# Sliding-window attention and SwiGLU on one core: an earlier first weight load, a rearranged start, and regrouped projection phases

## The chip, the cores and the metric

The kernel runs on one core of a Trainium2 chip. The metric is the device time of one launch in microseconds (us); smaller is better. "Before" is the kernel as it stood, "after" is the kernel with the change.

## The reference

The first half is causal attention with a window of 64 keys, for 8 batches, 8 heads, 576 tokens and a head size of 64. The second half is a SwiGLU block on the 4608 x 512 matrix of attention outputs, with a hidden size of 1536. All inputs and the output are float32.

```python
scores = q @ k.T / sqrt(64)                 # per batch and head
mask = (0 <= i - j) & (i - j < 64)
attn = softmax(where(mask, scores, -1e9))
x = (attn @ v) reshaped to (4608, 512)
g, val = x @ w_gate, x @ w_val              # 512 x 1536 each
out = (g * sigmoid(g) * val) @ w_out        # 1536 x 512
```

## The kernel before

The 4608 tokens are cut into nine tiles of 512, `t` = 0 to 8. Eight of them are the first 512 tokens of a batch. The ninth, `t` = `LAST` = 7, collects the last 64 tokens of all eight batches. Matmuls take bf16 operands and accumulate in float32 in PSUM.

Every tile passes through three steps.

*Attention.* Heads are taken in four pairs, `u` = 0 to 3. `scores(t, u)` makes the scores of a pair with small 64x64 matmuls (line 227), exponentiates them on ScalarE into `E` (line 233), and for `t` > 0 multiplies by a 0/1 mask on VectorE (line 235). `sums(t, u)` adds up the exponentials with two matmuls against a tile of ones (`totals`, line 245), and inverts the sum on ScalarE as exp(-ln(sum)) (lines 253 and 256). `values(t, u)` multiplies by the values with sixteen small matmuls (line 271) and scales the result by the inverse sum on VectorE into `xT` (line 277). `products` is `sums` and then `values`.

*Gate.* `gate_value(t, m)`, for `m` = 0 to 11, does four matmuls of 512 columns with `wg` into `g_ps` and four with `wv` into `v_ps` (line 306). `gate_end` applies SiLU on ScalarE (line 299) and multiplies on VectorE into `hT` (line 300). For `t` = 0 the first two `m` are done in parts by `gate_part` (line 286), one input chunk `c` at a time.

*Projection.* `project(t, s)`, for `s` = 0 to 3, does twelve matmuls of 512 columns with `wo` (line 315). `project_end` copies the result out of PSUM on VectorE (line 322), and SyncE stores it with four DMAs (line 334). For the last tile every other store is issued by ScalarE.

The order is written out by hand (`manual_schedule`): each engine executes its instructions in the order in which the program lists them. In the loop over `t`, the projection of tile `t` - 1 is woven into the attention of tile `t`: two `scores`, a `project`, two `scores`, a `project`, two `products`, a `project`, two `products`, a `project`. Then come the twelve `gate_value` of tile `t`. The text calls the woven part a projection phase.

ScalarE has two tables of functions to switch between: `set_exp` ahead of the scores, `set_silu` ahead of the gate.

The start has an order of its own (lines 351 to 538). Queries and keys of `t` = 0 come in float32 (`raw`), are cast to bf16 by `cast_first` (the table `casts` says which engine takes which; line 408), are turned by TensorE (`turn_pe`), and go through `scores(0, u)`. `keep_warm` puts dummy matmuls into TensorE's gaps. GpSimd casts, and it also issues most DMAs, all into one queue, in this order: two of the values of `t` = 0, the weights `wg` and `wv` in five steps each (`weights_gv`, line 160; with the casts of two value blocks, `cast_v`, after the first `wg`), four DMAs `q_s` with the queries of `t` = 1 (`load_qk(1)`, line 87), `wo` in three steps (`weights_o`, line 166), then values and more queries and keys. ScalarE issues four DMAs `k_f` with the keys of `t` = 1 during the gate of `t` = 0, casts them (`keys`, line 408), and TensorE turns them. The queries of `t` = 1 are turned on VectorE by `turn_q` (line 186), which needs all four `q_s`.

PSUM has four tags with two buffers each way: `a` (two buffers of two banks, for scores, some sums, values and turned keys), and `g` and `v` (two buffers of one bank each, for the gate, the sums of `t` > 0 in `v`, and projections in `g`).

Of the kernel before, what the change touches and what calls it, by code (L numbers as in the profile page):

```python
# [8 lines left out]
P = 128  # L9
FP32 = mybir.dt.float32  # L10
BF16 = mybir.dt.bfloat16
# [6 lines left out]
def kernel(  # L18
# [107 lines left out]
    def load_v(eng, dst, t, which=range(4)):  # L126
        for i in which:
            eng.dma_start(  # L128
                dst[:, i], v[batch(t), :, P * i:P * i + P].rearrange("h r d -> r h d")
            )  # L130
# [27 lines left out]
    def weights_gv(f0, f1, *which):  # L158
        for i in which or range(2):
            nc.gpsimd.dma_start(  # L160
                (wg, wv)[i][:, :, f0:f1],
                (moe_w_gate, moe_w_val)[i][:, f0:f1].rearrange("(c r) f -> r c f", r=P),
            )
# [79 lines left out]
    def totals(t, u, d_ps):  # L243
        for h in range(2):
            nc.tensor.matmul(  # L245
                d_ps[64 * h:64 * h + 64], ones[:, 0:D], weights[t, u][:, h, :]
            )

    def room(n):
        return fsb.tile([P, 2, 512], FP32, name="r", tag="r", bufs=4)[:, 0:n]  # L250

    def log(r, d_ps):
        nc.scalar.activation(r, d_ps, AF.Ln)  # L253

    def invert(r):
        nc.scalar.activation(r, r, AF.Exp, scale=-1.0)  # L256

    def sums(t, u, d_ps):
        totals(t, u, d_ps)
        r = room(1)[:, 0]  # L260
        log(r, d_ps)
        invert(r)
        inverse[t, u] = r

    def values(t, u, o_ps):
        E = weights.pop((t, u))
        if u == 0:
            xT[t] = att.tile([P, 4, 512], BF16, name="xT", tag="xT")
        for m in range(8):
            for h in range(2):  # L270
                nc.tensor.matmul(  # L271
                    blocks(o_ps[64 * h:64 * h + 64], t, m, m + 1),
                    (v1, v2)[m // 4][t % 2][:, m % 4, 2 * u + h, :] if t == LAST
                    else (v2, v1)[m % 2][t % 2][:, m // 2, 2 * u + h, :],
                    blocks(E[:, h, :], t, m, m + 1),
                )
        nc.vector.tensor_mul(xT[t][:, u, :], o_ps[:], inverse.pop((t, u)))  # L277

    def products(t, u):
        sums(t, u, ps_f.tile([P, 512], FP32, name="d_ps", tag="v")[:])  # L280
        values(t, u, ps_a.tile([P, 2, 512], FP32, name="ao_ps", tag="a")[:, 0])

    def gate_part(t, ms, tiles, c):
        for m, pair in zip(ms, tiles):
# [6 lines left out]
    def gate_tiles():  # L291
        return [ps_f.tile([P, 512], FP32, name=x + "_ps", tag=x) for x in "gv"]
# [43 lines left out]
    def out_tile():  # L336
        return ps_f.tile([P, 512], FP32, name="o_ps", tag="g")

    def project(t, s):
        o_ps = out_tile()  # L340
        project_part(t, (s,), (o_ps,), range(12))
        project_end(t, s, o_ps)

    def set_exp():
        nc.scalar.preload_act_table_set("natural_log_exp_and_others")

# [9 lines left out]
        load_runs(nc.scalar if u < 2 else nc.sync, raw[1][:, hs], k, 0, hs)  # L356
    load_v(nc.sync, staged[0, "v"], 0, (0, 1))
    set_exp()
    nc.vector.memset(ones[:], 1.0)
    make_identity(nc, identb[:])  # L360
    nc.vector.memset(zero[:], 0.0)
    for i in range(2):
# [3 lines left out]
    def keep_warm(n):  # L366
        for _ in range(n):
            nc.tensor.matmul(warm[0:D], ones[:, 0:D], ones[:])

    keep_warm(7)  # L370
    nc.gpsimd.memset(tri[:], 1.0)
    for a in range(2):
        half = tri[64 * a:64 * a + 64]
# [27 lines left out]
    def shift_dma(dst, src):  # L401
        nc.sync.dma_start(dst, src)

    def wide(name):
        return ps_a.tile([P, 2, 512], FP32, name=name, tag="a")

    def join(copy, dst, src):
        copy(dst.rearrange("r e (h d) -> r h e d", h=2), src)  # L408

    def one(name):  # L410
        return ps_a.tile([P, 2, 512], FP32, name=name, tag="a")[:, 0]

    casts = ((on_a, on_v), (on_p, on_v), (on_v, on_p), (on_p, on_p))

    def cast_first(u, i):
        join(casts[u][i], first[:, i, u], raw[i][:, 2 * u:2 * u + 2])

    def turn_pe(u):
        tps = [ps_f.tile([P, 512], BF16, name="tp", tag=x) for x in "gv"]
        for i in range(2):  # L420
            transposes(tps[i], first[:, i, u])
        (on_v if u else on_a)(queries[0][:, u, :], tps[0][:])
        split_k(kT[0][:, u, :], tps[1][:])
# [6 lines left out]
    load_v(nc.gpsimd, v1[0], 0, (2, 3))  # L430
    keep_warm(1)
    scores(0, 0)
    cast_first(2, 0)
    turn_pe(1)
    keep_warm(2)
    scores(0, 1)
    cast_first(2, 1)
    turn_pe(2)
    keep_warm(1)
    cast_first(3, 0)  # L440
    cast_first(3, 1)
    scores(0, 2)
    turn_pe(3)
    weights_gv(0, 256, 0)
    cast_v(0, (0, 1))
    weights_gv(0, 256, 1)
    weights_gv(256, 512)
    weights_gv(512, 768)
    weights_gv(768, 1280)
# [3 lines left out]
    weights_o(4, 8)  # L453
    weights_o(8, 12)
    load_v(nc.gpsimd, v1[1], 1)
    d_ps, r = wide("d_ps"), room(2)
    for u in range(2):
        totals(0, u, d_ps[:, u])
        inverse[0, u] = r[:, u]
    log(r, d_ps[:])  # L460
    scores(0, 3)
    invert(r)
    shift_v(0, on_v, 0, 2)
    shift_v(0, on_v, 2, 4)
    keep_warm(3)
    for u in (2, 3):
        d_ps = ps_f.tile([P, 512], FP32, name="d_ps", tag="gv"[u % 2])
        totals(0, u, d_ps[:])
        inverse[0, u] = room(1)[:, 0]
        log(inverse[0, u], d_ps[:])  # L470
    for u in (2, 3):
        invert(inverse[0, u])
    values(0, 0, one("ao_ps"))
    values(0, 1, one("ao_ps"))
    keep_warm(3)
    pairs = [gate_tiles() for _ in range(2)]
    values(0, 2, one("ao_ps"))
    gate_part(0, (0, 1), pairs, 0)
    values(0, 3, one("ao_ps"))
    for c in range(1, 4):  # L480
        gate_part(0, (0, 1), pairs, c)
    set_silu()
    raw_k = stage.tile([P, H, 4, D], FP32, name="k_f", tag="k")
    for m in range(12):
        if m < 2:
            gate_end(0, m, pairs[m])
        else:
            gate_value(0, m)
        if m == 2:
            for i in range(4):  # L490
                nc.vector.tensor_copy(
                    mask[:, 0, :, i], tri[:].rearrange("r c (x e) -> r e c x", e=16)
                )
            nc.vector.memset(mask[64:128, 0, :, 0, 0, :], 0.0)
            nc.vector.tensor_copy(mask[:, 1], mask[:, 0])
        if 3 <= m < 7:
            hs = slice(2 * m - 6, 2 * m - 4)
            load_runs(nc.scalar, raw_k[:, hs], k, 1, hs)
        if 7 <= m < 11:
            u = m - 7  # L500
            join(on_a, keys[:, u], raw_k[:, 2 * u:2 * u + 2])
        if m >= 8:
            u = m - 8
            tp = ps_a.tile([P, 512], BF16, name="tp", tag="a")
            transposes(tp, keys[:, u])
            split_k(kT[1][:, u, :], tp[:])
        if m >= 10:
            turn_q(1, m - 10)
    turn_q(1, 2)
    turn_q(1, 3)  # L510

    set_exp()
# [9 lines left out]
    for i in range(4):  # L522
        shift_v(1, on_v, i, i + 1)

    def d_tile():
        return ps_f.tile([P, 512], FP32, name="d_ps", tag="v")[:]

    for u in range(2):
        sums(1, u, d_tile())
    project(0, 2)  # L530
    o_ps = out_tile()
    for u in range(4):
        if u < 2:
            sums(1, u + 2, d_tile())
        values(1, u, one("ao_ps"))
        if u:
            project_part(0, (3,), (o_ps,), range(4 * u - 4, 4 * u))
    project_end(0, 3, o_ps)

    for t in range(1, NT):  # L540
        if t > 1:
            set_exp()
            for u in range(8):
                if u < 4:
                    scores(t, u)
                else:
                    products(t, u - 4)
                if u % 2:
                    project(t - 1, u // 2)
        set_silu()  # L550
        if t + 1 == LAST:
            load_last_v()
        elif t + 1 < NT:
            if t > 1:
                cast_v(t + 1)
            shift_v(t + 1, shift_dma)
        if t + 2 < NT:
            load_qk(t + 2)
            if t + 2 != LAST:
                stage_v(t + 2)  # L560
        if t == 2:
            k_l = load_k(
                cast.tile([P, 4, 4, 4 * D], BF16, name="k_l", tag="c0"),
                [(b, S - P) for b in range(4, 8)],
            )
            for b in range(8):
                nc.gpsimd.tensor_copy(
                    maskl[:, 0, :, b], tri[:, 1].rearrange("r (x e) -> r e x", e=16)
                )
            nc.gpsimd.tensor_copy(maskl[:, 1], maskl[:, 0])  # L570
        turns = (4, 6, 8, 10) if t == 1 else (1, 4, 7, 10)
        for m in range(12):
            gate_value(t, m)
            if m in turns and t + 1 < NT:
                turn(t + 1, turns.index(m))
            if m == 8 and 3 <= t < 7:
                turn_k(kT[2], k_l, t - 3)
    for s in range(4):
        project(NT - 1, s)

# [1 line left out]
_INS = ['q', 'k', 'v', 'moe_w_gate', 'moe_w_val', 'moe_w_out']  # L582
# [26 lines left out]
```

## Time and profile before

| | us |
|---|---|
| median of 7 runs | 338.07 (337.81 to 339.51) |
| the profiled execution's own time | 339.1 |
| its span in the profile | 337.3 |
| TensorE busy | 324.0 (96% of the span) |
| VectorE busy | 215.4 (64%) |
| ScalarE busy | 167.4 (50%) |
| GpSimd busy | 138.7 (41%) |
| mean granted TensorE clock | 0.994 of full speed |

The busy shares are averages over the span. The chain of waits, the idle time ahead of each instruction and the order of instructions in time tell more about a single stage. Times in those views are microseconds from the start of the span. In a row of the timeline, the first number is the start, the second the duration, `x` the number of instructions merged into the row, and the bracket at the end the idle time of the engine before the row and what ended it.

### The profile page before, as it was taken

The numbers are of one execution on the slowest core, as the hardware profiler recorded it, in microseconds if no ns is written. First come the engines' busy times: TensorE is split into PE (matmuls) and PEld (weight loads), VectorE is DVE, ScalarE is ACT, GpSimd is POOL, SyncE is SP. The second block draws the span as 40 slices with busy tenths as digits, with TensorE's granted clock in tenths as the row PEclk, the third lists the DMA queues.
The fourth block names the chain that finished last, engine by engine and source line by source line (L and its number), as shares of the span: only waits on it lengthen the run. The fifth ranks groups of instructions, "written<-read, shape, count | busy, mean of one in ns | idle before, by whom it ended". The sixth has DMA issues, their size and how long they took to land.

```text
span 337.3 us, 6930 instructions
## 1 busy us (share of the span) xinstructions
PE 324.0 (96%) x2683; PEld 154.2 (46%) x2729; DVE 215.4 (64%) x319; ACT 167.4 (50%) x238; POOL 138.7 (41%) x249
## 2 busy tenths in 40 slices
PE   7899799999999999999999999999999999999994
PEld 3544344444544454445444444444445444544441
DVE  6754747487767756786668656965786576744431
ACT  4844636337633664356535563475347633773300
POOL 5942535946875966246222996164200000000000
PEclk9999979999999999999999999999999999999999
DMA  7999999999999499729951999199501320010013
GB/s 254 178 200 235 218 187 223 133 190 217 149 254 207 46 160 230 148 31 219 173 114 12 157 182 178 12 179 182 121 0 41 80 62 3 21 74 31 3 32 93
DMA packets 83057, 44.12 MB, mean 131 GB/s; under 512 B 63824, under 2 KB 77648, under 8 KB 83024
## 3 DMA queue, kind: packets, MB, share of 16 engines
q0 software_dynamic: 49328, 22.56, 54.5%
q1 hardware_dynamic: 31680, 19.02, 20.6%
q10 hardware_dynamic: 2016, 2.10, 2.2%
q8 instruction: 21, 0.34, 0.4%
q14 instruction: 12, 0.10, 0.1%
HBM read 54.00 MB, written 9.44 MB: 188 GB/s over the span
## 4 chain that ended last, share of the span: by engine, by line
PE 82%; DMA 10%; POOL 3%; DVE 2%; issue 1%; ACT 1%; SPq 0%; DVEq 0%; POOLq 0%
PE o_ps L315 25%; PE v_ps L306 25%; PE g_ps L306 24%; DMA q_s<-in_q_dram 5%; PE s_ps L227 3%; PE d_ps L245 3%; DMA wv<-in_moe_w_val_dram 2%; PE ao_ps L271 2%; DMA q_f<-in_q_dram 1%; POOL qk_b L408 1%; POOL wg L160 1%; ACT E L233 1%; DMA out_dram<-os__4390 1%; POOL v L128 1%; DMA out_dram<-os__4428 1%
## 5 line engine op out<-in xcount | busy, mean ns | idle before, releaser
L299 ACT ACTIVATE sg<-g_ps 128x512 f32<-128x512 f32 x108 | 64.4, 597 | 115.1 <-PE g_ps L306 81.6
L300 DVE TENSOR_TENSOR hT<-sg,v_ps 128x512 bf16<-128x512 f32 x108 | 74.8, 693 | 63.3 <-PE v_ps L306 61.3
L306 PE MATMUL v_ps<-xT,wv 128*128 128x512 bf16 x418 | 108.3, 379 | 0.4
L306 PE MATMUL g_ps<-xT,wg 128*128 128x512 bf16 x412 | 107.5, 379 | 0.5
L315 PE MATMUL o_ps<-wo,hT 128*128 128x512 bf16 x405 | 98.1, 384 | 1.8 <-issue 0.8
L107 POOL DMA_DIRECT2D k_s<-in_k_dram x112 | 60.5, 550 | 29.0 <-DMA q_s<-in_q_dram 20.9
L306 PEld LDWEIGHTS <-wv 128*128 128x128 bf16 x424 | 41.4, 98 | 50.2 <-DMA wv<-in_moe_w_val_dram 0.5
L306 PEld LDWEIGHTS <-wg 128*128 128x128 bf16 x424 | 41.4, 98 | 49.5 <-issue 0.3
L315 PEld LDWEIGHTS <-hT 128*128 128x128 bf16 x432 | 39.9, 99 | 46.4 <-issue 2.6
L233 ACT ACTIVATE E<-s_ps 128x1024 bf16<-128x1024 f32 x36 | 35.2, 1021 | 11.9 <-PE s_ps L227 11.8
L277 DVE TENSOR_TENSOR xT<-ao_ps,r 128x512 bf16<-128x512 f32 x36 | 24.6, 690 | 20.9 <-ACT r L256 18.1
L196 DVE STREAM_TRANSPOSE kT<-k_s 128x512 bf16<-128x512 bf16 x28 | 35.9, 1283 | 0.0
L253 ACT ACTIVATE r<-d_ps 128x512 f32<-128x512 f32 (+1 forms) x35 | 20.9, 602 | 21.0 <-PE d_ps L245 20.9
L235 DVE TENSOR_TENSOR E<-E,mask 128x1024 bf16<-128x1024 bf16 x28 | 21.8, 784 | 13.0 <-ACT E L233 12.9
L87 POOL DMA_DIRECT2D q_s<-in_q_dram x28 | 15.3, 556 | 27.0 <-DVE qT L186 16.6
L186 DVE STREAM_TRANSPOSE qT<-q_s 128x512 bf16<-128x512 bf16 x32 | 22.3, 702 | 1.2 <-DMA q_s<-in_q_dram 1.2
L256 ACT ACTIVATE r<-r 128x512 f32<-128x512 f32 (+1 forms) x35 | 22.4, 643 | 1.0
L148 POOL CAST v<-v_f 128x512 bf16<-128x512 f32 x22 | 14.0, 657 | 19.8 <-DMA v_f<-in_v_dram 14.8
L271 PEld LDWEIGHTS <-v 128*64 128x64 bf16 x576 | 14.0, 112 | 5.0 <-issue 1.5
L271 PE MATMUL ao_ps<-E,v 128*64 128x64 bf16 x576 | 15.2, 195 | 0.1
L245 PE MATMUL d_ps<-E,ones 128*64 128x512 bf16 x72 | 14.3, 392 | 0.6 <-ACT E L233 0.3
L227 PE MATMUL s_ps<-qT,kT 64*64 64x128 bf16 (+1 forms) x640 | 12.4, 211 | 0.4 <-DVE kT L177 0.2
(94 smaller groups left out, 174.4 us busy)
## 6 DMA issues: line engine op xcount, KB each, us to landing
q_s<-in_q_dram POOLq DMA_DIRECT2D x28, 248.0 KB, 6.8
k_s<-in_k_dram POOLq DMA_DIRECT2D x112, 56.0 KB, 5.0
v_f<-in_v_dram SPq DMA_DIRECT2D x22, 256.0 KB
v<-in_v_dram POOLq DMA_DIRECT2D x18, 128.0 KB, 5.6
k_f<-in_k_dram ACTq DMA_DIRECT2D x6, 256.0 KB
wo<-in_moe_w_out_dram POOLq DMA_DIRECT2D x3, 512.0 KB, 15.3
v<-v SPq DMA_DIRECT2D x6, 256.0 KB
v<-v SPq DMA_DIRECT2D x6, 192.0 KB
```

Source lines behind the costliest of these rows:

```text
L107: nc.gpsimd.dma_start(k_s[p0:p0 + 32, g, :, 0:w], k[b, a:H:2, s:s + P].rearrange("u (r e) d -> r u (e d)", e=4) [:, :, 32 * c:32 * c + w],)
L196: nc.vector.transpose(dst[:, u, :].rearrange("r (g x e) -> r g e x", g=4, e=4), k_s[:, :, u].rearrange("r g (e d) -> r g e d", d=D)[:, :, ...
L227: nc.tensor.matmul(blocks(s_ps[64 * c:64 * c + 64, h], t, lo, hi), zero[r] if src is None else src[r, u, x:x + 64], blocks(qT[r], t, lo, h ...
L233: nc.scalar.activation(E[:], s_ps[:], AF.Exp, scale=0.125)
L245: nc.tensor.matmul(d_ps[64 * h:64 * h + 64], ones[:, 0:D], weights[t, u][:, h, :])
L256: nc.scalar.activation(r, r, AF.Exp, scale=-1.0)
L271: nc.tensor.matmul(blocks(o_ps[64 * h:64 * h + 64], t, m, m + 1), (v1, v2)[m // 4][t % 2][:, m % 4, 2 * u + h, :] if t == LAST else (v2, v ...
L277: nc.vector.tensor_mul(xT[t][:, u, :], o_ps[:], inverse.pop((t, u)))
L299: nc.scalar.activation(sg[:], g_ps[:], AF.Silu)
L300: nc.vector.tensor_mul(hT[t][:, m, :], sg[:], v_ps[:])
L306: nc.tensor.matmul(ps[:], w[:, c, P * m:P * m + P], xT[t][:, c, :], start=(c == 0), stop=(c == 3),)
L315: nc.tensor.matmul(o_ps[:], hT[t][:, c, P * s:P * s + P], wo[:, c, :], start=(c == 0), stop=(c == 11),)
```

## The change

In the start:

- The first memset of `ones` is split, and the seven dummy matmuls of 512 columns become six of 128 columns and six of 512.
- `casts` is redistributed. Of the eight casts of queries and keys, ScalarE had one, VectorE three and GpSimd four; now ScalarE has four, VectorE two and GpSimd two. The calls of `cast_first` stand at other places between `scores` and `turn_pe`.
- `weights_gv(0, 256)` issues both `wg` and `wv` ahead of `cast_v`. All the DMA issues now stand ahead of `scores(0, 2)` in the program's text; engine by engine, only GpSimd's own order matters for them.
- The inverse of the sums of pairs 0 and 1 stands ahead of the exponential of pair 3. Values of pairs 0 and 1 are multiplied as soon as their inverse is there, in buffers of `g` and `v`, and the first `gate_part` (chunk 0, which is pair 0) stands ahead of the values of pairs 2 and 3.
- The four loads of the keys of `t` = 1, their casts and their transposes stand two steps `m` earlier in the gate of `t` = 0, and the four `turn_q(1, u)` one step earlier.

In the projection phases, `values` is split into `mix` (the matmuls) and `scale` (the multiplication on VectorE). `finish_values` does the sums of pairs 2 and 3, then the four `mix`, then the four `scale`, with two wide buffers of tag `a` for the four results. A phase is now: two `scores`, a `project`, two `scores`, two `sums`, two `project`, `finish_values`, a `project`. The phase of `t` = 1 ends in the same way.

At the end, the last `project` is done by `project_last`, in two halves of 256 columns, each with its own copy and four stores.

```diff
+    def mix(t, u, o_ps):         # values() without its last line
+        E = weights.pop((t, u))
         for m in range(8):
...
+    def finish_values(t):
+        for u in (2, 3):
+            sums(t, u, d_tile())
+        tiles = wide("ao_ps"), wide("ao_ps")
+        for u in range(4):
+            mix(t, u, tiles[u // 2][:, u % 2])
+        for u in range(4):
+            scale(t, u, tiles[u // 2][:, u % 2])
...
+    def project_last(t, s):
+        rows = out[S * batch(t):S * batch(t) + 512].rearrange("(r e) f -> e r f", e=16)
+        os_ = fsb.tile([P, 512], FP32, name="os_", tag="os_", bufs=3)
+        tiles = out_tile(), out_tile()
+        for x in range(2):
+            f = slice(256 * x, 256 * x + 256)
+            for c in range(12):
+                nc.tensor.matmul(
+                    tiles[x][:, 0:256], hT[t][:, c, P * s:P * s + P], wo[:, c, f],
+                    start=(c == 0), stop=(c == 11),
+                )
+            nc.vector.tensor_copy(os_[:, f], tiles[x][:, 0:256])
+            for i in range(4):
+                eng = nc.scalar if i % 2 else nc.sync
+                eng.dma_start(rows[4 * s + i][:, f], os_[32 * i:32 * i + 32, f])
...
-    nc.vector.memset(ones[:], 1.0)
+    nc.vector.memset(ones[:, 0:P], 1.0)
+    nc.vector.memset(ones[:, P:512], 1.0)
...
-    keep_warm(7)
+    for _ in range(6):
+        nc.tensor.matmul(warm[0:D, 0:P], ones[:, 0:D], ones[:, 0:P])
+    keep_warm(6)
...
-    casts = ((on_a, on_v), (on_p, on_v), (on_v, on_p), (on_p, on_p))
+    casts = ((on_a, on_v), (on_p, on_a), (on_a, on_p), (on_v, on_a))
...
     scores(0, 0)
+    turn_pe(1)
     cast_first(2, 0)
-    turn_pe(1)
+    cast_first(2, 1)
     keep_warm(2)
     scores(0, 1)
-    cast_first(2, 1)
+    cast_first(3, 0)
+    cast_first(3, 1)
     turn_pe(2)
     keep_warm(1)
-    cast_first(3, 0)
-    cast_first(3, 1)
-    scores(0, 2)
-    turn_pe(3)
-    weights_gv(0, 256, 0)
+    weights_gv(0, 256)
     cast_v(0, (0, 1))
-    weights_gv(0, 256, 1)
     weights_gv(256, 512)
...
     load_v(nc.gpsimd, v1[1], 1)
+    scores(0, 2)
+    turn_pe(3)
     d_ps, r = wide("d_ps"), room(2)
...
     log(r, d_ps[:])
+    invert(r)
     scores(0, 3)
-    invert(r)
...
-    keep_warm(3)
-    for u in (2, 3):
-        d_ps = ps_f.tile([P, 512], FP32, name="d_ps", tag="gv"[u % 2])
-        totals(0, u, d_ps[:])
-        inverse[0, u] = room(1)[:, 0]
-        log(inverse[0, u], d_ps[:])
+
+    def log_of(u):
+        d_ps = one("d_ps")
+        totals(0, u, d_ps)
+        inverse[0, u] = room(1)[:, 0]
+        log(inverse[0, u], d_ps)
+
+    keep_warm(5)
+    log_of(2)
+    for u in range(2):
+        values(0, u, ps_f.tile([P, 512], FP32, name="ao_ps", tag="gv"[u])[:])
+    log_of(3)
+    pairs = [gate_tiles() for _ in range(2)]
+    gate_part(0, (0, 1), pairs, 0)
     for u in (2, 3):
         invert(inverse[0, u])
-    values(0, 0, one("ao_ps"))
-    values(0, 1, one("ao_ps"))
-    keep_warm(3)
-    pairs = [gate_tiles() for _ in range(2)]
     values(0, 2, one("ao_ps"))
-    gate_part(0, (0, 1), pairs, 0)
+    gate_part(0, (0, 1), pairs, 1)
     values(0, 3, one("ao_ps"))
-    for c in range(1, 4):
+    for c in (2, 3):
         gate_part(0, (0, 1), pairs, c)
...
-        if 3 <= m < 7:
-            hs = slice(2 * m - 6, 2 * m - 4)
+        if 1 <= m < 5:
+            hs = slice(2 * m - 2, 2 * m)
             load_runs(nc.scalar, raw_k[:, hs], k, 1, hs)
-        if 7 <= m < 11:
-            u = m - 7
+        if 5 <= m < 9:
+            u = m - 5
             join(on_a, keys[:, u], raw_k[:, 2 * u:2 * u + 2])
-        if m >= 8:
-            u = m - 8
+        if 6 <= m < 10:
+            u = m - 6
...
-        if m >= 10:
-            turn_q(1, m - 10)
-    turn_q(1, 2)
+        if m >= 9:
+            turn_q(1, m - 9)
     turn_q(1, 3)
...
     project(0, 2)
-    o_ps = out_tile()
-    for u in range(4):
-        if u < 2:
-            sums(1, u + 2, d_tile())
-        values(1, u, one("ao_ps"))
-        if u:
-            project_part(0, (3,), (o_ps,), range(4 * u - 4, 4 * u))
-    project_end(0, 3, o_ps)
+    finish_values(1)
+    project(0, 3)
...
-            for u in range(8):
-                if u < 4:
-                    scores(t, u)
-                else:
-                    products(t, u - 4)
-                if u % 2:
-                    project(t - 1, u // 2)
+            for u in range(4):
+                scores(t, u)
+                if u == 1:
+                    project(t - 1, 0)
+            for u in range(2):
+                sums(t, u, d_tile())
+            for s in (1, 2):
+                project(t - 1, s)
+            finish_values(t)
+            project(t - 1, 3)
...
-    for s in range(4):
+    for s in range(3):
         project(NT - 1, s)
+    project_last(NT - 1, 3)
```

More of the change, by code (lines that the diff above doesn't have):

```diff
@@ L263, in sums @@
         inverse[t, u] = r
-    def values(t, u, o_ps):
+    def mix(t, u, o_ps):
         E = weights.pop((t, u))
-        if u == 0:
-            xT[t] = att.tile([P, 4, 512], BF16, name="xT", tag="xT")
         for m in range(8):
@@ L276, in values, with scale, wide, d_tile @@
                 )
[L277 to L281, printed above, removed]
+    def scale(t, u, o_ps):
+        if u == 0:
+            xT[t] = att.tile([P, 4, 512], BF16, name="xT", tag="xT")
+        nc.vector.tensor_mul(xT[t][:, u, :], o_ps, inverse.pop((t, u)))
+    def values(t, u, o_ps):
+        mix(t, u, o_ps)
+        scale(t, u, o_ps)
+    def wide(name):
+        return ps_a.tile([P, 2, 512], FP32, name=name, tag="a")
+    def d_tile():
+        return ps_f.tile([P, 512], FP32, name="d_ps", tag="v")[:]
+    def finish_values(t):
[6 more added lines that the diff above has]
+            scale(t, u, tiles[u // 2][:, u % 2])
     def gate_part(t, ms, tiles, c):
@@ L402, in shift_dma @@
         nc.sync.dma_start(dst, src)
-    def wide(name):
-        return ps_a.tile([P, 2, 512], FP32, name=name, tag="a")
     def join(copy, dst, src):
@@ L523 @@
         shift_v(1, on_v, i, i + 1)
-    def d_tile():
-        return ps_f.tile([P, 512], FP32, name="d_ps", tag="v")[:]
     for u in range(2):
```

## The prediction

> **What bounds the kernel now.** I read the page first (TensorE busy 96%, so only its idle time, its clock and its order can be won), then the waits of TensorE, longest first:
>
> ```profile
> PE s_ps L227 <- DVE qT L186: 2.1, 2, 1.4
> PE warm L368 <- DVE ones L359: 1.5, 1, 1.5
> PE o_ps L315 <- issue: 0.8, 5, 0.2
> PE v_ps L286 <- DMA wv<-in_moe_w_val_dram: 0.5, 1, 0.5
> ```
>
> The only long wait is for the turned queries of t = 1. The timeline of TensorE shows it, and what follows it:
>
> ```profile
> 40.11 0.22 PE L227 MATMUL s_ps<-qT,zero 64*64 64x64 bf16 x2 [0.77 <-DVE qT L186]
> ...
> 41.90 0.22 PE L227 MATMUL s_ps<-qT,zero 64*64 64x64 bf16 x2 [1.37 <-DVE qT L186]
> ...
> 43.05 3.66 PE L315 MATMUL o_ps<-wo,hT 128*128 128x512 bf16 x9 [0.19 <-issue]
> ```
>
> Nine 512-column matmuls take 3.66; elsewhere they start every 0.216. The table by windows gives a granted clock of 0.50 from 42.8 to 46.2. Twelve matmuls took from 42.26 to 46.63 = 4.37 instead of 2.60: 1.77 lost. What is late behind the wait is told by the chain of waits for 10 to 44 us:
>
> ```profile
> 11.64 0.68 POOL wv L160
> ...
> 14.66 8.41 DMA wv<-in_moe_w_val_dram
> 23.07 0.28 issue
> 23.35 15.87 DMA q_s<-in_q_dram
> ```
>
> The start is bounded by GpSimd's DMA queue, not by an engine: weights, then q_s, then wo land one after another. q_s lands at 39.22, wo in three steps at 41.34, 43.92 and 46.42. A projection phase later on has no wait; here the limit is the order on TensorE:
>
> ```profile
> 117.57 2.54 PE L315 MATMUL o_ps<-wo,hT 128*128 128x512 bf16 x11 [0.16 <-issue]
> 120.04 0.41 PE L245 MATMUL d_ps<-E,ones 128*64 128x512 bf16 x2
> 120.28 0.42 PE L271 MATMUL ao_ps<-E,v 128*64 128x64 bf16 x16
> 120.53 0.39 PE L245 MATMUL d_ps<-E,ones 128*64 128x512 bf16 x2
> 120.75 0.42 PE L271 MATMUL ao_ps<-E,v 128*64 128x64 bf16 x16
> 121.10 2.76 PE L315 MATMUL o_ps<-wo,hT 128*128 128x512 bf16 x11
> ```
>
> Single starts: the last full matmul at 119.73, d_ps at 120.04, 0.310 instead of 0.216, so **entering** small tiles costs 0.09. The last ao_ps starts at 120.97, o_ps at 121.10 and the next at 121.33: 0.128 and 0.227 instead of 0.028 and 0.216, so **leaving** costs 0.11.
>
> [...] half clock for 3.41 us, after 3.4 us in which TensorE was idle for 2.1. [...] from 29 to 33 us GpSimd's queue moved 552 packets and ScalarE's (k_f) 460, 245 GB/s together; from 22 to 26 GpSimd's alone made 206. [...] one mask multiplication (two SBUF inputs) took 3.0 us instead of the median 0.69, from 83.49, while four GpSimd casts ran (83.68 to 85.95). [...]
>
> **The change, part by part.**
>
> *First weights.* GpSimd loses the casts that stood at 8.61 and 9.16 (0.55 each): the first wg issues at 8.6 instead of 9.72. The first wv (11.58) no longer follows the two value casts (1.11): 9.35. Everything behind issues 1.1 earlier; the value casts move from 10.47 to 10.1, covered by VectorE, which reaches their shift only at 12.07. Worth: the queue ran at 64 GB/s from 13.0 to 14.5, against 189 right after, waiting for that wv. That hole, 1.5 x (1 - 64/189) = 1.0 us, closes. All behind it lands 1.0 earlier: q_s 38.2, wo 40.3, 42.9, 45.4.
>
> *Three casts on ScalarE* (0.62 each) fit its gaps of 0.85, 0.94 and 0.83 ahead of the exponentials: nothing. If a cast were 0.3 late, so would be one exponential, inside the slack below.
>
> *Inverse ahead of the last exponential, gate part on pair 0.* The inverse (1.06) pushes that exponential from 12.72 to 13.7 and its end to 14.75; five dummy matmuls and the values of pairs 0 and 1 cover it on TensorE. xT of pair 0 is ready at about 15.2, the first wv lands near 15.6 (16.53 before), and the sixteen matmuls and two values (4.1 us) end near 19.7 instead of 20.4. Gain 0.7, but not kept: q_s decides later.
>
> *Keys of t = 1 two steps earlier.* The four k_f issues move from 23.3-28.5 to about 19.5-24.2, and share with wv's 512 KB step, which landed at 28.35, 0.1 us ahead of its use. From about 22 on, some 660 KB of weights go at about 118 instead of 200 KB/us: 5.6 instead of 3.3. It lands near 29.6 although its start is 1.0 earlier, and TensorE, there at 27.5, waits about 2.1 at m = 6. Bounds: 27.5 (k_f starts late, no wait) to 31.7 (k_f goes first altogether, 1 MB at 235 KB/us). Behind that wait stand 10.4 us of gate work (28.40 to 38.8 before), so scores(1, 0) begin at 40.0; earliest by q_s 38.2 + 0.85 = 39.1. turn_q(1, 1) now waits for one hT less a key copy: 2.0 after q_s instead of 2.6, 40.2. Then scores until 40.7 and twelve o_ps: wo's second step at 42.9 and third at 45.4 hold them. The last eight matmuls after 45.4 (1.73) end at 47.2, against 49.9 in the trace: **2.7**, of which 1.77 is the half clock.
>
> *Phase of t = 1.* Three visits to small tiles become one: 2 x (0.09 + 0.11) = **0.4**.
>
> *Seven phases.* Four visits become three: 0.20. Scores to sums is a new change of tile shape; at 12.29 such a step took 0.14 instead of 0.03, so minus 0.10. Three sum-to-value steps (0.024 each) go: plus 0.05. Net 0.15, x 7 = **1.05** (-0.35 to 1.75 if that step costs 0.2 more, or nothing). Two waits are new. Sums of pair 1 follow the scores of pair 3 directly and need mask 1: it ends 3.82 after the phase starts (3.99 once), they come at 4.07: no stall by 0.1 to 0.25; behind them stand two project. The gate needs the last scale: ln, exp, ln, exp (2.45) and scale end 3.6 after the first sum of pair 2, the gate comes at 4.1. Cover: the last project (2.6).
>
> *Tail.* After the last matmul at 332.8 came a copy of 0.69 and the stores. A copy of half the columns is about 0.4 by that row (not under 0.35); stores half as large save at most 0.2; the extra twelve matmuls nothing to 0.05. **0.3.** Earlier dummies (0.36) are hidden: the first transposes wait for q and k, cast at 4.19 and 4.61.
>
> Sum: 2.7 + 0.4 + 1.05 + 0.3 = 4.45. Own time 339.1 - 4.45 = 334.65. The profiled execution stands 1.03 above the median of 338.07; I put that to the half-clock stretch[...]. The changed kernel has none in this case, so its median is 334.7 as well: 3.4 below the median before.
>
> **Rivals.**
> 1. *The wait moves to m = 6 and halves the clock there.* [...] 1.77 lost, of which 0.8 was spare ahead of wo: 335.7. Chance 0.2.
> 2. *The 1.03 belongs to profiling, and plain runs have the half clock too.* For: seven runs lie within 1.7. Then the whole 4.45 counts: 333.6. Chance 0.1.
> 3. *Nothing at the start.* k_f merely takes the hole's place, wo lands as before, the seven phases save nothing (their low bound): the tail's 0.3 and half of the 0.4 of t = 1 are left, 0.5, 337.6, within 0.2%. This also holds the case that the DMA order doesn't bring the weights earlier. Chance 0.07.
> 4. *Slower: sums meet a stretched mask.* A mask 1 of 3.0 us would end 2.1 after its sums are due, and TensorE has nothing in between; two project stood there before. For: it happened to mask 2 at t = 2. Against: casts met a mask in full once in eight phases. It decides from two such meetings on: 4.2 eats the gain of 3.4 and more, 338.9; three make 341. Chance 0.06.
>
> **Numbers.** Forecast 0.57, rivals 0.2, 0.1, 0.07 and 0.06. About 0.2% (0.68 us) is what a measurement here can tell from no change. Faster is the forecast with rivals 1 and 2: 0.87; same 0.07; slower 0.06. The range of 332.9 to 336.6 holds these three cases, with 0.7 below rival 2 and 0.9 above rival 1 for the bounds of the phases and of wv.
>
> **What would show it.** Right: first wg issue near 8.6, no hole at 13-14.5, q_s landed near 38.2, a wait on wv at m = 6, no half clock near 43, first d_ps of t = 1 near 47.2, phase period 34.65 instead of 34.80, tail 0.3 shorter. Wrong: q_s landing at 39 or later; a wait of d_ps on E in the phases; a half-clock stretch; a period that didn't shrink.

## The result and the profile after

The changed kernel takes 334.68 us (median of 12 runs, 333.96 to 335.58). The kernel before, run beside it, takes 338.74 (31 runs, 337.06 to 341.83). The ratio is 0.9876 with a 95% interval of 0.9856 to 0.9897: some 4.2 us faster. The forecast was 334.7 in a range of 332.9 to 336.6. The profiled execution has a span of 332.8 (337.3 before), 334.67 with what lies around it (339.1 before).

TensorE's waits in the changed kernel, from the list of waits (who waited for whom: us in total, times, longest):

```profile
PE warm L405 <- DVE ones L392: 1.1, 1, 1.1
PE o_ps L332 <- DMA wo<-in_moe_w_out_dram: 0.7, 1, 0.7
PE ao_ps L269 <- DVE v L156: 0.6, 1, 0.6
PE v_ps L303 <- DMA wv<-in_moe_w_val_dram: 0.4, 1, 0.4
PE g_ps L303 <- DVE xT L279: 0.4, 1, 0.4
PE s_ps L227 <- DVE qT L186: 0.3, 1, 0.3
```

The wait for turned queries fell from 2.1 to 0.3, and behind the first dummy matmuls the longest wait is now for wo. The timeline of TensorE across that place:

```profile
39.11 0.22 PE L227 MATMUL s_ps<-qT,zero 64*64 64x64 bf16 x2
...
39.87 0.22 PE L227 MATMUL s_ps<-qT,zero 64*64 64x64 bf16 x2 [0.34 <-DVE qT L186]
...
40.31 1.90 PE L332 MATMUL o_ps<-wo,hT 128*128 128x512 bf16 x7
42.89 1.02 PE L332 MATMUL o_ps<-wo,hT 128*128 128x512 bf16 x4 [0.67 <-DMA wo<-in_moe_w_out_dram]
...
47.33 0.62 PE L245 MATMUL d_ps<-E,ones 128*64 128x512 bf16 x4
```

In the kernel before, the row of these first sums was:

```profile
49.92 0.62 PE L245 MATMUL d_ps<-E,ones 128*64 128x512 bf16 x4
```

The first sums of t = 1 stand at 47.33 instead of 49.92, the clock is full up to the last matmul, and in this stretch TensorE stops for more than 0.4 only where the second step of wo lands (42.85). The chain of waits confirms that the queue of weights still bounds the start; its pieces with wo:

```profile
15.39 12.90 DMA wv<-in_moe_w_val_dram
28.29 0.28 issue
28.57 14.28 DMA wo<-in_moe_w_out_dram
42.85 0.04 issue
```

GpSimd's part of the timeline, with its DMA issues, shows the first edit. The first wv follows the first wg directly, at 9.28 instead of 11.58:

```profile
7.98 0.63 POOL L441 CAST qk_b<-k_f 128x512 bf16<-128x512 f32 x1
8.53 0.76 POOL L160 DMA_DIRECT2D wg<-in_moe_w_gate_dram  x1
9.28 0.76 POOL L160 DMA_DIRECT2D wv<-in_moe_w_val_dram  x1
10.14 0.61 POOL L148 CAST v<-v_f 128x512 bf16<-128x512 f32 x1
11.02 0.61 POOL L148 CAST v<-v_f 128x512 bf16<-128x512 f32 x1 [0.27 <-DMA v_f<-in_v_dram]
11.58 0.74 POOL L160 DMA_DIRECT2D wg<-in_moe_w_gate_dram  x1
```

The second wg follows at 11.58 (12.31 before). It comes 0.7 earlier and not 1.1, since the second value cast waits for its load until 11.02.

What the DMA engines moved from 10 to 20 us, first in the kernel before, then in the changed one:

```profile
DMA packets 4882, 1.65 MB, mean 165 GB/s; under 512 B 2260, under 2 KB 4881, under 8 KB 4881
```

```profile
DMA packets 5268, 1.91 MB, mean 191 GB/s; under 512 B 2170, under 2 KB 5267, under 8 KB 5267
```

0.26 MB more in the same ten microseconds, at 191 GB/s, are 1.4 us of the queue. A whole projection phase (t = 4) on TensorE, to be set beside the one that the prediction shows:

```profile
148.90 0.62 PE L245 MATMUL d_ps<-E,ones 128*64 128x512 bf16 x4
149.45 5.36 PE L332 MATMUL o_ps<-wo,hT 128*128 128x512 bf16 x23
154.74 0.62 PE L245 MATMUL d_ps<-E,ones 128*64 128x512 bf16 x4
155.19 1.18 PE L269 MATMUL ao_ps<-E,v 128*64 128x64 bf16 x64
156.31 2.76 PE L332 MATMUL o_ps<-wo,hT 128*128 128x512 bf16 x11
158.91 1.03 PE L323 MATMUL g_ps<-xT,wg 128*128 128x512 bf16 x4
```

Two projections run in one piece (23 of 24 matmuls are recorded, without a break), the sums and all four values in another, and the gate follows without a wait. From gate to gate a tile takes 34.69 to 34.71 instead of 34.80 (one of 34.81 instead of 34.90).

The two profiled executions differ by 4.46 in span. By stage, read from single starts: 2.59 up to the first sums of t = 1; 0.45 from there to the gate of t = 1 (7.49 instead of 7.93); 0.73 in the seven phases (gate of t = 1 to gate of t = 8: 242.97 instead of 243.70); 0.73 behind the last matmul (from its end to the end of the span 3.75 instead of 4.48). Together these are 4.50; the last projection, longer by 0.04, takes the rest back.

### The profile page after: what moved, and what is told of

The parts are those of the page before. It is cut to its first block, busy times and chain, and to the rows that moved or that the text cites. A ratio compares the mean times of both kernels' runs of the same rounds, so it can differ in the third digit from the quotient of the medians.

```text
span 332.8 us, 6959 instructions
## 1 busy us (share of the span) xinstructions
PE 322.3 (97%) x2702; PEld 154.7 (46%) x2745; DVE 211.6 (64%) x320; ACT 168.2 (51%) x241; POOL 138.5 (42%) x247
## 4 chain that ended last, share of the span: by engine, by line
PE 85%; DMA 11%; POOL 1%; issue 1%; DVE 0%; SPq 0%
PE o_ps L332 27%; PE g_ps L323 25%; PE v_ps L323 24%; DMA wo<-in_moe_w_out_dram 4%; DMA wv<-in_moe_w_val_dram 4%; PE s_ps L227 3%; PE d_ps L245 3%; PE ao_ps L269 2%; DMA v_f<-in_v_dram 2%; DMA k_f<-in_k_dram 1%; PE o_ps L368 1%; POOL wg L160 1%; POOL wv L160 0%; POOL v L148 0%; DVE os__4423 L372 0%
## 5 line engine op out<-in xcount | busy, mean ns | idle before, releaser
L323 PE MATMUL v_ps<-xT,wv 128*128 128x512 bf16 x414 | 107.1, 379 | 0.2
L332 PE MATMUL o_ps<-wo,hT 128*128 128x512 bf16 x396 | 93.9, 380 | 2.2 <-DMA wo<-in_moe_w_out_dram 0.7
L332 PEld LDWEIGHTS <-hT 128*128 128x128 bf16 x420 | 39.1, 98 | 49.0 <-issue 4.6
L253 ACT ACTIVATE r<-d_ps 128x512 f32<-128x512 f32 (+1 forms) x35 | 21.1, 602 | 17.8 <-PE d_ps L245 17.6
L235 DVE TENSOR_TENSOR E<-E,mask 128x1024 bf16<-128x1024 bf16 x28 | 20.1, 722 | 11.9 <-ACT E L233 11.9
L279 DVE TENSOR_TENSOR xT<-ao_ps,r 128x512 bf16<-128x512 f32 x36 | 22.5, 683 | 6.2 <-PE ao_ps L269 6.2
L87 POOL DMA_DIRECT2D q_s<-in_q_dram x28 | 15.2, 555 | 23.2 <-DVE qT L186 12.9
L94 POOL DMA_DIRECT2D q_s<-in_q_dram x16 | 8.6, 628 | 9.5 <-DVE qT L186 9.5
L269 PEld LDWEIGHTS <-v 128*64 128x64 bf16 x576 | 10.9, 112 | 3.3 <-issue 0.8
```

The costliest lines, as they stand in the source:

```text
L279: nc.vector.tensor_mul(xT[t][:, u, :], o_ps, inverse.pop((t, u)))
L323: nc.tensor.matmul(ps[:], w[:, c, P * m:P * m + P], xT[t][:, c, :], start=(c == 0), stop=(c == 3),)
L332: nc.tensor.matmul(o_ps[:], hT[t][:, c, P * s:P * s + P], wo[:, c, :], start=(c == 0), stop=(c == 11),)
```

## The experiments

Each kernel was run with the kernel before on the same chip. Ratios are to the kernel before, with 95% intervals; stage times are from the kernel's own profile. The kernel before stood at 338.68 beside e1 to e4, 338.40 beside e5 to e8 and 338.89 beside e9 to e12. The changed kernel was not timed beside them, so a comparison with its 334.68 or its ratio of 0.9876 goes across groups of runs.

**e1_start: the start alone.** The changed kernel with old phases and old tail.

```diff
-            for u in range(4):
-                scores(t, u)
-                if u == 1:
-                    project(t - 1, 0)
...
+            for u in range(8):
+                if u < 4:
+                    scores(t, u)
+                else:
+                    sums(t, u - 4, d_tile())
+                    values(t, u - 4, one("ao_ps"))
+                if u % 2:
+                    project(t - 1, u // 2)
...
-    for s in range(3):
+    for s in range(4):
         project(NT - 1, s)
-    project_last(NT - 1, 3)
```

> All edits of the start, with the projection phases and the last projection as before. Theory: the start gives its part alone; the first sums of t = 1 stand near 47.3 us in the profile as in the changed kernel (49.92 before), there is no half-clock stretch near 43, and the median falls by 2 to 2.7. Rival (the start merely works together with the regrouped phases): under 1.5.

Measured: 336.17, ratio 0.9929 (0.9911 to 0.9947), 2.4 us. First sums at 47.04, gate of t = 1 at 54.97, full clock, phases of 34.80 as before. The start gives its part without the phases.

**e2_phases: the phases alone.** The kernel before with `finish_values` and the new loop.

```diff
...
-                else:
-                    products(t, u - 4)
...
+            for u in range(2):
+                sums(t, u, d_tile())
+            for s in (1, 2):
+                project(t - 1, s)
+            finish_values(t)
+            project(t - 1, 3)
```

> Only the regrouped phases (t = 1 included). Theory: gate to gate 34.71 instead of 34.81 in seven phases and 0.45 at t = 1, together 1.1 to 1.2; the wait for the queries of t = 1 and a half clock stay. Rival (the phases gain 0.2 or more each, and the start less): over 1.8. With the half clock coming and going, the median may scatter by 1.

Measured: 337.22, ratio 0.9961 (0.9949 to 0.9974), 1.3 us. Gate to gate 34.69 to 34.71, and 7.49 from the first sums of t = 1 to its gate, as in the changed kernel. With e1 and the 0.7 of the tail (from the profiles) this makes 4.4, within the intervals the whole of 4.2: the parts add up. A surprise stands in its profile: the old start, with the waits for queries of 0.90 and 1.36, and no half clock.

**e3_warm: the half clock taken away.** Dummy matmuls in those two waits of the kernel before.

```diff
     for u in range(4):
+        for _ in range((4, 7, 0, 0)[u]):
+            nc.tensor.matmul(halves[0][0:D], ones[:, 0:D], ones[:])
         scores(1, u)
```

> The kernel before, with eleven dummy matmuls of 512 columns added in TensorE's two waits for the queries of t = 1 (four ahead of the scores of pair 0, seven ahead of pair 1). They add no needed work. Theory: the half clock after these waits is a cost of its own, up to 1.77; with it gone the median falls by 1 to 1.8, and the runs scatter less than those before. The limit is the second and third step of wo at 43.9 and 46.4: first sums of t = 1 at 48.2 or a little more. Rival 2 of the prediction turned round (the half clock is seldom, the median doesn't contain it): no change within 0.4.

Measured: 338.14, ratio 0.9988 (0.9975 to 1.0002), by itself inconclusive on whether there is any gain, but not the 1 to 1.8 of the theory: the low end of the interval is 0.85 us. The clock is full in its profile up to the last matmul, and the first sums stand at 49.14.

The mean granted clock of every single run says more. In the profiles without a half-clock stretch ahead of the last matmul it is 0.997 to 1.0; with one stretch (the kernel before) it is 0.994, with two (e8) 0.99. Runs at 0.995 or less are counted here as runs with a stretch:

| | with a stretch | their median | median of the others |
|---|---|---|---|
| kernel before, beside e1 to e12 | 39 of 95 | 339.32 | 338.17 |
| e3 | 1 of 22 | 340.83 | 338.11 |
| changed kernel | 0 of 12 | | 334.68 |

(One run of the kernel before, at 342.30, is left aside.) So the half clock is no rarity of one profile. It comes in some two of five runs of the kernel before, which are 1.15 us slower than the others (0.85 to 1.33 when the runs are resampled). The mean doesn't tell where in a run the stretch lies, but dummies in the two waits for queries, and nowhere else, took away nearly all of them. e3 stands where the kernel before stands without a stretch. For the median that is worth about 0.5 (338.68 to 338.14), less than the theory's 1 to 1.8, since most runs had nothing to lose.

**e11_before_a and e12_before_b: the kernel before twice more,** for its profile, without an edit.

> The kernel before once more, for its profile. Theory: the half clock near 43 comes in some executions and not in others, with the same waits ahead of it. If it is absent here, the first sums of t = 1 stand near 48.2 to 49.1 instead of 49.92. Rival: it is there each time, 3.4 us long, and the sums stand at 49.9.

> The same as the run before, a second time: one more execution in which the half clock near 43 is there or not.

Measured: own times 338.76 and 338.81, no half clock near 43 in either, and yet the first sums at 49.58 and 49.63. What was late there is in the lists of waits, of the first and then of the second:

```profile
PE v_ps L306 <- DMA wv<-in_moe_w_val_dram: 1.6, 1, 1.6
PE s_ps L227 <- DVE qT L186: 1.6, 2, 1.4
```

```profile
PE v_ps L286 <- DMA wv<-in_moe_w_val_dram: 1.9, 1, 1.9
PE s_ps L227 <- DVE qT L186: 1.6, 2, 1.4
```

Weights. The last step of wo landed at 47.72 and 47.77, against 46.42 in the first profile, and 45.47 in the changed kernel. Neither the theory (48.2 to 49.1) nor the rival holds. So the kernel before varies in two things, in whether its clock halves and in when its weights come, and the one profile that the prediction had was an execution with early weights and a half clock.

**e4_weights: one edit of the start on the kernel before.**

```diff
-    weights_gv(0, 256, 0)
+    weights_gv(0, 256)
     cast_v(0, (0, 1))
-    weights_gv(0, 256, 1)
```

> The kernel before, with only the first wv issued ahead of the two value casts. Theory: wv issues near 10.5 instead of 11.6, the hole in the DMA queue at 13 to 14.5 closes by most of its 1.0, and q_s lands near 38.3 instead of 39.2; the wait for the queries ends 0.9 earlier, and the median falls by 0.5 to 1. Rival (the keys of t = 1 and the order of turning decide, not the hole): q_s lands at 39 or later, under 0.3.

Measured: 337.53, ratio 0.9974 (0.996 to 0.9988), 0.9 us. wv issues at 10.52 instead of 11.58, q_s lands at 38.67 and wo at 45.70; the first sums stand at 47.69. The gain lies inside the theory's 0.5 to 1, and issue and wo moved as it says (wo by 0.7 against the first profile). q_s, forecast at 38.3 by the theory and at 39 or later by the rival, lies between them. An issue one microsecond earlier, on a queue with a hole behind it, was worth most of a microsecond.

**e6_weights_back: the same edit undone in the changed kernel.**

```diff
-    weights_gv(0, 256)
+    weights_gv(0, 256, 0)
     cast_v(0, (0, 1))
+    weights_gv(0, 256, 1)
```

> The changed kernel with the first wv behind the two value casts again. GpSimd still has two casts fewer than before. Theory: wv issues near 10.4 instead of 9.3, only part of the hole comes back, since the first packets of wg don't go out before 11.5 in either: q_s and wo land 0 to 0.5 later, the median is 0 to 0.5 slower. Rival (the early wv is what carries the start): 0.9 to 1 slower.

Measured: 335.83, ratio 0.9923 (0.9901 to 0.9945; the changed kernel 0.9876), about 1.2 us slower in medians and 1.6 by the ratios. The rival won, with help: wv issues at 11.42 and not at 10.4, as the two casts wait for v_f (0.45 and 0.28), and wo's last step lands at 46.36. The wait that the prediction saw at m = 6 is here:

```profile
PE v_ps L323 <- DMA wv<-in_moe_w_val_dram: 0.9, 1, 0.9
PE o_ps L332 <- DMA wo<-in_moe_w_out_dram: 0.7, 2, 0.4
```

**e5_late_keys: the keys and queries of t = 1 at their old places.**

```diff
-        if 1 <= m < 5:
-            hs = slice(2 * m - 2, 2 * m)
+        if 3 <= m < 7:
+            hs = slice(2 * m - 6, 2 * m - 4)
...
-        if m >= 9:
-            turn_q(1, m - 9)
+        if m >= 10:
+            turn_q(1, m - 10)
+    turn_q(1, 2)
     turn_q(1, 3)
```

> The changed kernel with the keys of t = 1 loaded, cast and turned, and the queries turned, at their old places in the gate of t = 0. The first weights stay early. Theory: the order of turning is worth 0.6 behind the landing of q_s (pair 1 is turned 2.6 after it instead of 2.0), and TensorE waits 0.7 to 1.3 for pair 1 again, which may halve the clock; wo's steps then hide part of it: slower than the changed kernel by 0.3 to 0.6, and in executions with a half clock by up to 2. q_s lands within 0.3 of the changed kernel's 37.8, since the same bytes go through. Rival (the early keys only share the weights' bandwidth and cost): faster than the changed kernel.

Measured: 334.78, ratio 0.9887 (0.986 to 0.9914). In medians no difference from the changed kernel can be told; in the profile the first sums stand 0.54 later (47.87), with 1.58 of wait for pair 1, and q_s at 37.98. It is in line with the theory in size, but only the profile shows it.

**e10_old_first_gate: the first gate part in its old place.**

```diff
-    keep_warm(5)
-    log_of(2)
-    for u in range(2):
-        values(0, u, ps_f.tile([P, 512], FP32, name="ao_ps", tag="gv"[u])[:])
-    log_of(3)
...
+    keep_warm(3)
+    for u in (2, 3):
+        log_of(u)
+    for u in (2, 3):
+        invert(inverse[0, u])
+    values(0, 0, ps_f.tile([P, 512], FP32, name="ao_ps", tag="g")[:])
+    values(0, 1, ps_f.tile([P, 512], FP32, name="ao_ps", tag="v")[:])
+    keep_warm(3)
...
```

> The changed kernel with values and first gate parts of t = 0 in the old order (values of pairs 0 and 1, dummies, values of pair 2, gate part 0, values of pair 3, the other parts). Theory: the first wv (landing near 16.3 in the changed kernel) starts the gate in either order, and sixteen matmuls and the values behind it last the same: the gate of m = 2 starts within 0.4 of the changed kernel's 20.86, the median within 0.3. Rival (the forecast's 0.7 was there and covers something): slower by 0.5 or more.

Measured: 334.46, ratio 0.9868 (0.984 to 0.9896), the same as the changed kernel. The gate of m = 2 starts at 20.68, against 20.86. This edit is worth nothing that can be measured here: the first wv, landing at 16.34 (changed) and 16.49 (e10), starts the gate in either order.

**e7_plain_tail: the last projection in one piece.**

```diff
-    for s in range(3):
+    for s in range(4):
         project(NT - 1, s)
-    project_last(NT - 1, 3)
```

> The changed kernel with the last projection as before, in one piece. Theory: 0.3 from the shorter copy (0.42 instead of 0.69) and 0.3 from the smaller last stores, so the time from the last matmul's end to the end of the span is 4.5 instead of 3.75: 0.6 to 0.75 slower. Rival (0.3, as the prediction had it; the rest is scatter of the end of a launch): 0.3 slower.

Measured: 335.14, ratio 0.99 (0.9874 to 0.9926). In the profile the end of the span comes 4.47 after the last matmul (3.75 changed, 4.48 before): 0.72. The medians say 0.5, and five runs don't settle the size.

**e8_v_sync: an attempt to relieve the queue.** All values of t = 0 go through SyncE in float32.

```diff
-    load_v(nc.sync, staged[0, "v"], 0, (0, 1))
+    load_v(nc.sync, staged[0, "v"], 0)
...
-    load_v(nc.gpsimd, v1[0], 0, (2, 3))
...
     weights_gv(256, 512)
+    cast_v(0, (2, 3))
```

> The changed kernel with all four value blocks of t = 0 loaded by SyncE in float32 and cast by GpSimd, so that GpSimd's queue begins with the weights. Theory: DMA bytes in GpSimd's queue decide the start; without the 256 KB in packets of 128 bytes (2.2 us in the profile before) the weights, q_s and wo land about 1 earlier, TensorE's waits for wo (0.67) and wv (0.41) go: faster than the changed kernel by 0.3 to 0.9. Rival: the values come later on the other queue and the first gate starts later (values of pair 0 behind 14.4): slower by 0.5 or more.

Measured: 337.83, ratio 0.9983 (0.9966 to 1.0): the rival. Values came late, GpSimd (busy for 1.70 of the 6.0 us from 14 to 20) waited with its casts and so with the weights behind them, and TensorE waited 5.5 us for values, with the clock at half from 16.9 to 23.7. The profiled execution is the slowest of the 22, but 19 of them have a mean clock of 0.995 or less. Its longest wait, and the table by windows for 16.9 to 23.7 (its last three figures are the granted clock, 0.50, the DMA share, 0.81, and the GB/s):

```profile
PE ao_ps L269 <- DVE v L156: 5.5, 1, 5.5
```

```profile
16.90:23.70 6.80, 3.71 (x46) 1.89 (x48) 1.88 (x4) 2.67 (x4) 5.12 (x8) 0.50 0.81 101
```

**e9_sums_early: work without wo ahead of wo.**

```diff
-        if u % 2:
-            project_part(0, (0, 1), halves, range(3 * u - 3, 3 * u + 3))
+        if u == 1:
+            project_part(0, (0, 1), halves, range(0, 4))
+    for u in range(2):
+        sums(1, u, d_tile())
+    project_part(0, (0, 1), halves, range(4, 12))
```

> The changed kernel, with the sums of pairs 0 and 1 of t = 1 moved ahead of chunks 4 to 11 of the first two projections (the first part takes chunks 0 to 3 instead of 0 to 5). Theory: between 39 and 47 us the changed kernel is held by wo's second and third steps (42.85, 45.47), so work that needs no wo fits ahead of them for nothing; the sums (0.45) and one visit to small tiles (0.2) leave the stretch behind, and the gate of t = 1 starts 0.5 to 0.7 earlier than 54.81: faster than the changed kernel by 0.5 to 0.7. Rival (wo doesn't hold TensorE, the order only shifts the wait): within 0.2.

Measured: 334.43, ratio 0.9873 (0.9842 to 0.9905), the same as the changed kernel. Its waits tell why:

```profile
PE o_ps L332 <- DVE os__770 L339: 0.6, 1, 0.6
PE o_ps L332 <- DMA wo<-in_moe_w_out_dram: 0.6, 1, 0.6
```

The sums did leave the stretch behind wo. But they had covered VectorE's copies of the first two projections; now the third projection stands behind those copies and waits 0.56 for a buffer of tag `g`. A new wait took the place of the saved visit: the gate of t = 1 starts 9.34 after the last step of wo lands (54.48 and 45.14), as in the changed kernel (54.81 and 45.47).

No version beat the changed kernel beyond the intervals: 334.43 (e9), 334.46 (e10) and 334.68 are the same time.

## Why the prediction was right, point by point

**The sum was right, and so was the time**: 4.45 forecast, 4.43 between the two profiled executions (339.1 and 334.67), and 334.7 for a median of 334.68. Its terms were less right than their sum, and that they met so closely is luck: the phases gave 0.32 less than forecast and the tail 0.43 more, and against the other two profiles of the kernel before (338.76 and 338.81) the difference would have been 4.1.

- *The start, 2.7 forecast, 2.59 in the profiles.* The chain was right: the hole behind the late wv closes (194 GB/s from 13.0 to 14.5, 64 before), q_s lands at 37.78 (38.2 forecast), wo at 40.27, 42.85 and 45.47 (40.3, 42.9, 45.4), the first sums stand at 47.33 (47.2). e4 and e6 show the worth of the early wv by itself, 0.9 and 1.2 to 1.6. What gives the rest of e1's 2.4 was not separated: e5 and e10 find nothing in the medians for the keys and the gate part, and the redistributed casts, which bring the first wg from 9.72 to 8.53, were not run alone. The issues behind the first wv came 0.7 earlier and not 1.1, which the full queue hid. The hole is larger than the 1.0 read from one execution, some 1.4 to 2.5 by when the queue's first 2 MB were out (22.5 to 23.5 with the old start, 21.0 to 21.1 with the new).
- *The half clock, 1.03 on one execution and none on the median by forecast.* The step from own time to median, "I put that to the half-clock stretch", was right in kind, as runs with a stretch are 1.15 slower (1.03 assumed), and the changed kernel has none in 12 runs. It was wrong in how often: not one execution, but 39 of 95. Against the runs without a stretch the changed kernel gains 3.5 (338.17 to 334.68), the 3.4 of the forecast; against the median of 31 runs, 338.74, it gains 4.1. That the median of the first seven runs, 338.07, stood where the runs without a stretch stand was luck. "Of which 1.77 is the half clock" holds for the one profile and is too much for most runs. A likely reason, not shown, is that the half clock and late weights hide each other: wo's last step landed at 46.4 to 47.8 in five executions with the old start (before, e2, e3, e11, e12), against 45.1 to 45.5 in six with the new (the changed kernel, e1, e5, e7, e9, e10), and where it is late the first sums stand at 49.1 to 49.6 with a full clock too (e3, e11, e12; 49.92 with the half clock).
- *The wait at m = 6, 2.1 forecast, did not come.* wv landed at 28.29 and was used at 28.62. The mis-sized terms are the times of k_f: its first issue came at 20.64, not 19.5, and its first packet at 24.2, not 22. Until then wv had the queue alone. From 24 to 31 the two queues did share: 1221 packets of GpSimd's queue and 1038 of ScalarE's, at 251 GB/s together. GpSimd's 0.74 MB of that are 106 KB/us, where the author's estimate for the weights was 118. With wv issued later again, in e6, the wait was there (0.94), so its place was right and the slack was 0.33 us (28.62 less 28.29).
- *The first gate part, "gain 0.7, but not kept", was -0.4.* The gate of m = 2 began at 20.86 instead of 20.50. The first wv was taken to land near 15.6 and landed at 16.34, only 0.2 earlier than before though issued 2.3 earlier; and the stretch from there to the gate took 4.5, not 4.1. In e7 and e9 wv did land at 15.6, and the gate of m = 2 began at 20.12 and 20.16, a gain of 0.4. Neither the loss nor the gain shows in the medians (e10, e7, e9), as the prediction said of its gain: the end of the start is set by q_s and wo.
- *The phases, 1.05 forecast, 0.73.* Per phase 0.10 instead of 0.15. The signs and places were right: one visit less; scores to sums took 0.116 from start to start, 0.09 more than inside the scores. The two new waits stayed covered: no d_ps waits for E in the phases, and the gate waits for no xT.
- *t = 1: 0.4 forecast, 0.45 measured* (0.45 in e2).
- *The tail: 0.3 forecast, 0.73 in the profiles.* The copy took 0.42 instead of 0.69, as forecast. From the copy's end to the last DMA packet it was 1.75 instead of 2.04 (0.29 less, where the author's estimate for the smaller stores was at most 0.2), and the close of the span behind it 1.53 instead of 1.71, which the prediction didn't count; part of that may be scatter. e7 repeats the 0.72.
- *The rivals.* Rival 1 (half clock at m = 6) fell with the wait; that the wait would halve the clock there was the author's estimate, and was not shown. Rival 2 (plain runs have the half clock too and gain the whole 4.45) was right in part: some two of five have it, and the gain on medians, 4.1, lies between the 3.4 of the forecast and its 4.45. Its number for the changed kernel, 333.6, was wrong. Rival 3 fell with e4. Rival 4: no mask of pair 1 met the casts in the changed profile. Two other masks did, at t = 3, and took 1.15 and 1.09 instead of 0.69. The meeting wasn't provoked, so its price stays untested.

## What to carry to other kernels

Where a queue of loads bounds the start, look for the moment at which it runs empty, and move what delays that one issue; what stands behind it gains (here about 1 us for the swap of two lines). Visits to short matmuls in another tile shape had a price here (three instead of four gave 0.10 a phase), so gather them, but ask what each visit was hiding: e9 shows one that covered two copies. And one profile is one execution: count how often a striking loss in it comes. The half clock stood in one of three profiles of the kernel before, and three profiles can be read as rule or as exception; the mean clock of 95 runs said two of five.

## What the hardware showed that was not expected

- *Half clock after some waits and not after others.* In the kernel before, TensorE was busy for 1.36 of the 3.50 us from 39.3 to 42.8, so idle for 2.1, with the waits of 0.77 and 1.37 for queries in it, and the granted clock was 0.50 for the 3.41 us from 42.77. In e2, waits of 0.90 and 1.36 for the same queries, and in e11, waits of 0.23 and 1.36, were followed by full clock. So nearly the same waits went with a loss of 1.77 in one execution and with none in another. What decides between them was not shown.
- *How much the landing of a load varies.* The first loads of wg and wv move in 512 packets of 512 bytes each. Counted so, over all 16 DMA engines together, the first wv's last packet was out at 14.48 in the changed kernel and at 15.81 before, and the load landed at 16.34 and 16.53, 1.86 and 0.72 later. In five more executions of the new start (e1, e5, e7, e9, e10) the packets were out at 14.45 to 14.53 as well, and the load landed at 15.57 to 16.49. So the same load landed up to 0.92 earlier or later with its packets out within 0.08 of each other; what sets that stays open. The packets of this load came 1.3 earlier than before, its landing in the profiled pair only 0.2.
- *How late a second queue begins.* The first packet of k_f moved 3.5 us after its issue, on engines busy with GpSimd's queue (3.6 in the kernel before). At the start of the span it was 1.6 (1.8 in the kernel before).
